# Batch 0 of a fused attention and gated-MLP kernel: split fp32r products in place of plain fp32 products

## The chip, the cores and the metric

The kernel runs on one core of one Trainium2 chip. The metric is the device time of one execution in microseconds (us), as the median of several runs of the same program.

## The reference

Eight batches; q, k and v are given per batch for 8 heads, 576 positions and 64 channels. Each batch goes through an attention that adds two parts, and the sum, with heads side by side as 512 channels, goes through a gated MLP with a residual:

```python
out_d = sm_attn(q_d, k_d, v_d)                    # q, k, v averaged over groups of 4 positions
mask = np.abs(pos[:, None] - pos[None, :]) < 4    # the local part: a band
...
x = repeat(out_d, 4) + softmax_band(q, k) @ v     # (8, 576, 512)
h = gelu_tanh(x @ w_in)                           # w_in: 512 x 1024
u, v = h[..., :512], h[..., 512:]
v_n = (v - mu) / np.sqrt(var + 1e-06) * g_ln
v_s = np.einsum('ts,bsd->btd', w_sg, v_n) + b_sg[None, :, None]
return x + (u * v_s) @ w_out                      # w_out: 512 x 512
```

The two large weights arrive as 64-bit floats and are turned into fp32 on the chip.

## The kernel before, in words

**Units of work.** The attention of a batch is done for four pairs of heads, so there are 32 pairs, numbered g = 4b + p. Pair g leaves its result in a tile of 128 channels by 576 positions, `x`, in the transposed form that the MLP needs; pair p of a batch is also slice k = p of the MLP's 512 input channels. The MLP of a batch has these products on TensorE: `v` (five blocks of positions, s = 0 to 4, the last of 64 positions; 512 columns), `u` (eight blocks of 288 columns), `s` (the product with w_sg) and `o` (the product with w_out).

**Split products.** A product of fp32 accuracy is made of fp32r matmuls: each operand is cut into a high part (a cast to fp32r) and a low part (the value minus its high part, again fp32r), and high by high, high by low and low by high are added in PSUM. For `x` this is `x_high` (task `xh`, ScalarE or VectorE), `x_low` (`xl`, VectorE or GpSimd, two SBUF inputs) and `x_last` (`xc`, which puts the low part of the last 64 positions behind the high part, so that the last block of `v` needs two matmuls per slice and not three). For a weight it is `high` (`wh`) and `low` (`wl`), behind the steps that make fp32 out of the 64-bit words: `scaled` and `units` (`wq`, `wu`, ScalarE), `shift` (`wb`, two VectorE operations) and `total` (`wt`, GpSimd).

**Batch 0.** Before the change, batch 0 has no `xh`, `xl` and `xc`. Its `v` and `u` take the plain fp32 `x` and the plain fp32 weights, as `total` leaves them (line 937 for `v`, line 1156 for `u`); such a matmul shows as two records in the trace. The weights are split all the same, but only batch 1 reads the parts. So that TensorE can begin before all four pairs of batch 0 are there, its `v` is cut into one task per slice: `vk`s`.`k for k = 0 to 2, and `v0.`s for k = 3. From batch 1 on, `v` runs on line 944 and `u` through `product` (line 1145).

**Order of the work.** A task list (name, engine, what it must follow, buffers) is written out by hand in Python, and a long string, `ORDER`, gives the order of all tasks; `/P`, `/V`, `/A` behind a name put it on GpSimd, VectorE or ScalarE in place of its usual engine. Each engine runs its tasks in that order and waits by semaphores. Other task names used below: `S`, `Y`, `YS` scores; `mx`, `my` row maxima; `ia`, `ib` scores minus their maximum; `ea`, `eb`, `ec` exponentials; `np`, `nq` the division by the row sums; `T`, `U`, `t` transposes; `D` the product with v; `qs`, `ks`, `vs` sums over four positions; `od`, `xa`, `xb` the sum of the two parts into `x`; `vg`, `vb`, `vp`, `vn`, `vh`, `vl` the GELU, the statistics, the root, the normalisation and the split of v. Where `vl` is done for all five blocks of batch 0, the first `s` product of batch 0 can start.

The program opens with 28 matmuls on zeros ahead of `S0` and has 20 more ahead of `S3`.

```python
if first:                                   # batch 0, in v_mm
    for k in ks:
        l = sb[k]["x"][:, s * P:min(S, (s + 1) * P)]
        nc.tensor.matmul(out=acc[0:LEFT] if last else acc, lhsT=l, rhs=unsplit(f"y{k}"), start=k == 0, stop=k == KT - 1)
    return
ops = []                                    # every other batch
for k in ks:
    xh, xl = sb[k]["xh"][:, ts], None if last else sb[k]["xl"][:, ts]
    ops += [(xh, 0, k), (xh, 1, k)] + ([] if last else [(xl, 0, k)])
```

Of the kernel before, what the change touches and what calls it, by code (L numbers as in the profile page):

```python
# [1540 lines left out]
```

## Time and profile before

| what | value |
|---|---|
| time, median of 3 runs | 547.8 us (546.92 to 550.19) |
| the profiled execution's own time | 548.28 us |
| its span, first to last instruction | 546.5 us |
| TensorE busy | 538.8 us (99% of the span) |
| VectorE busy | 461.3 us (84%) |
| ScalarE busy | 423.9 us (78%) |
| GpSimd busy | 346.0 us (63%) |

The busy times come from one profiled execution. TensorE's matmuls are pipelined and their ends are modelled, so its busy share says that it had work, not that it ran at its peak; where it says that TensorE is busy, the start of one matmul after another is the better measure. Shares over the whole span are averages over stages that have different limits.

### The profile page before, as it was taken

Reading aid. Unit: us, or ns where it says so; the run is one execution under the profiler, and the core shown is the slowest. Engines: PE = TensorE matmul, PEld = TensorE weight load, DVE = VectorE, ACT = ScalarE, POOL = GpSimd, SP = SyncE. Lnnn points to the kernel's source line nnn. Section 1 sums busy time; section 2 is a strip of 40 time slices with the busy share of each in tenths; the row PEclk is TensorE's granted clock in tenths of the full one; section 3 lists DMA queues with packets and bytes.
Section 4 is the critical chain, followed back from the end, with each engine's and each line's share of the span. In section 5 each row is a group of like instructions: output and inputs, shape, how many; then the busy total and the mean of one; then the engine's idle time right before and its main releaser. Section 6 shows DMA issues by size and latency. Waiting matters only on the chain.

```text
span 546.5 us, 17297 instructions
## 1 busy us (share of the span) xinstructions
PE 538.8 (99%) x6725; PEld 490.4 (90%) x6725; DVE 461.3 (84%) x994; ACT 423.9 (78%) x1447; POOL 346.0 (63%) x419
## 2 busy tenths in 40 slices
PE   9899999999999999999999999999999999999997
PEld 6746689899998999989998999989999899989997
DVE  5998999998889887897878888996998888975785
ACT  3999999798998987789797988797884987736320
POOL 6888878776796587576585654536545665544514
PEclk9999999999999999999999999999999999999999
DMA  8799466502443252303524242222435013200103
GB/s 308 209 313 321 163 185 199 172 23 58 137 124 90 88 189 76 111 24 110 168 79 148 63 147 97 68 80 81 150 110 183 3 57 131 75 1 1 67 0 109
DMA packets 31841, 64.47 MB, mean 118 GB/s; under 512 B 3728, under 2 KB 4752, under 8 KB 31760
## 3 DMA queue, kind: packets, MB, share of 16 engines
q1 hardware_dynamic: 31760, 63.38, 37.3%
q8 instruction: 53, 0.87, 0.7%
q14 instruction: 28, 0.23, 0.1%
HBM read 53.92 MB, written 9.44 MB: 116 GB/s over the span
## 4 chain that ended last, share of the span: by engine, by line
PE 90%; DMA 5%; ACT 2%; DVE 1%; SPq 1%; issue 0%; ACTq 0%
PE ps L1145 22%; PE ps L1099 17%; PE ps L944 16%; PE ps L1280 14%; PE ps L813 3%; PE ps L829 3%; PE ps L752 3%; PE ps L937 3%; PE ps L645 3%; PE ps L761 2%; PE ps L666 2%; DMA weight_y<-in_w_in_dram 2%; PE ps L1156 2%; DMA weight_z<-in_w_in_dram 1%; DMA R<-in_qT_dram 1%; SPq L240 1%
## 5 line engine op out<-in xcount | busy, mean ns | idle before, releaser
L1145 PE MATMUL ps<-X,weight_z 128*128 128x288 f32 x448 | 95.3, 298 | 0.3 <-issue 0.3
L705 ACT ACTIVATE X<-X,nb 128x64 f32<-128x64 f32 x280 | 93.6, 339 | 0.5
L944 PE MATMUL ps<-weight_y,X 128*128 128x512 f32 x280 | 85.0, 397 | 0.4 <-ACT R L963 0.4
L1145 PEld LDWEIGHTS ps<-X,weight_z 128*128 128x128 f32 x448 | 73.6, 188 | 0.7 <-issue 0.5
L1145 PE MATMUL ps<-R,weight_z 128*128 128x288 f32 x224 | 66.0, 295 | 0.0
L944 PEld LDWEIGHTS ps<-weight_y,X 128*128 128x128 f32 x280 | 51.1, 188 | 11.2 <-ACT R L963 0.7
L1099 PE MATMUL ps<-wsg_h,R 128*128 128x288 f32 x266 | 57.7, 299 | 0.0
L1287 DVE TENSOR_TENSOR R<-ps,R 128x288 f32<-128x288 f32 x98 | 42.0, 450 | 14.9 <-PE ps L1280 14.4
L705 ACT ACTIVATION_READ_ACCUMULATOR X<-X,nb 128x1 f32 x280 | 53.4, 191 | 0.0
L1280 PE MATMUL ps<-R,weight_r 128*128 128x288 f32 x336 | 49.6, 296 | 0.0
L248 ACT CAST R<-R 128x512 fp32r<-128x512 f32 (+2 forms) x68 | 42.5, 641 | 7.2 <-POOL R L1054 3.9
L1280 PEld LDWEIGHTS ps<-R,weight_r 128*128 128x128 f32 x336 | 46.2, 188 | 0.7
L944 PE MATMUL ps<-weight_y,R 128*128 128x512 f32 x112 | 44.1, 394 | 0.0
L1099 PEld LDWEIGHTS ps<-wsg_h,R 128*128 128x128 f32 x266 | 43.6, 188 | 0.3
L248 ACT COPY R<-ps 112x288 f32<-112x288 f32 (+4 forms) x93 | 32.2, 391 | 14.3 <-PE ps L944 5.5
L1145 PEld LDWEIGHTS ps<-R,weight_z 128*128 128x128 f32 x224 | 42.2, 188 | 0.0
L1263 POOL TENSOR_TENSOR R<-R,R 128x576 fp32r<-128x576 f32 x18 | 26.3, 1472 | 23.4 <-DVE R L248 13.5
L741 POOL TENSOR_TENSOR X<-X,rc 128x640 f32<-128x640 f32 x22 | 28.8, 1309 | 15.7 <-DVE rc L738 15.6
L1179 ACT ACTIVATE R<-ps 128x288 f32<-128x288 f32 x64 | 24.3, 411 | 18.3 <-PE ps L1145 16.7
L1280 PE MATMUL ps<-R,R 128*128 128x288 f32 x252 | 37.4, 297 | 0.0
L727 ACT ACTIVATE pd<-ps,nbd 128x144 f32<-128x144 f32 x96 | 35.4, 377 | 1.1 <-DVE nbd L696 0.5
L1280 PEld LDWEIGHTS ps<-R,R 128*128 128x128 f32 x252 | 34.8, 188 | 0.9
(223 smaller groups left out, 1643.7 us busy)
## 6 DMA issues: line engine op xcount, KB each, us to landing
R<-in_v_dram SPq DMA_DIRECT2D x60, 224.0 KB, 3.0
X<-in_vw_dram SPq DMA_DIRECT2D x32, 320.0 KB, 4.4
R<-in_qT_dram SPq DMA_DIRECT2D x32, 293.0 KB, 3.8
R<-in_kT_dram SPq DMA_DIRECT2D x32, 293.0 KB, 3.2
out_dram<-R SPq DMA_DIRECT2D x28, 288.0 KB, 3.0
R<-in_w_sgT_dram SPq DMA_DIRECT2D x10, 288.0 KB, 5.3
weight_y<-in_w_in_dram SPq DMA_DIRECT2D x4, 512.0 KB, 6.2
weight_z<-in_w_in_dram SPq DMA_DIRECT2D x4, 512.0 KB, 6.4
```

The lines of the kernel that those rows point to most:

```text
L248: (nc.scalar.copy if e == "A" else ENG[e].tensor_copy)(**kw)
L645: nc.tensor.matmul(out=sp[i][os, c * KB:(c + 1) * KB], lhsT=q[hs, t * QB:t * QB + KB], rhs=k[hs, t * QB:t * QB + KB], start=not early, sto ...
L705: nc.scalar.activation(out=st["ms"][:, t, :], in_=src, func=AF.Exp, bias=st["nb"][:, t:t + 1], scale=scale, accum_out=sums[par][:, t:t + 1])
L727: nc.scalar.activation(out=pd[:, n], in_=st["sdv"][n].rearrange("p (c k) -> p c k", c=3), func=AF.Exp, bias=st["nbd"][:, n:n + 1], scale=s ...
L741: ENG[e].tensor_tensor(out=st["ms"], in0=st["ms"], in1=bc_last(st["rc"][:, 0:NT], KB), op=ALU.mult)
L944: nc.tensor.matmul(out=acc, lhsT=r32(l), rhs=r32(weights[f"y{k}"][:, 0, w]), start=(i == 0 and ks[0] == 0), stop=(i == len(ops) - 1 and ks ...
L1099: nc.tensor.matmul(out=s_bank(j, c), lhsT=r32(l), rhs=r32(r), start=first_in and i == 0, stop=i == len(ops) - 1, skip_group_check=not firs ...
L1145: nc.tensor.matmul(out=acc[:, 0:HALF], lhsT=r32(l), rhs=r32(r), start=(first and n == 0), stop=(last and n == len(ops) - 1))
L1179: nc.scalar.activation(out=gate(i), in_=at["ps", "m", b, "u", i][:, 0:HALF], func=AF.Gelu_apprx_tanh)
L1263: ENG[e].tensor_tensor(out=r32(gl[m]), in0=us[raws[m]], in1=gh[m], op=ALU.subtract)
L1280: nc.tensor.matmul(out=bank(j, c), lhsT=r32(l), rhs=r32(r), start=first and i == 0, stop=i == len(ops) - 1, skip_group_check=not first)
L1287: nc.vector.tensor_tensor(out=x, in0=bank(j, c), in1=x, op=ALU.add)
```

## The change

Batch 0 is treated like the other batches. `unsplit` and the three branches for batch 0 (in `v_mm`, `v_act` and `u_mm`) go; the early return that kept `xh`, `xl` and `xc` from pairs 0 to 3 goes; `v` of batch 0 waits for `xl` and `wly`, its `u` for `xl` and `wlz`; the last block of its `v` gets the copy and the addition (`va`, `vj`) that the other batches have. `ORDER` is written anew, all 32 pairs and all batches of it. Fourteen tasks are new: `xh0` to `xh3`, `xl0` to `xl3`, `xc0` to `xc3`, `va0.4` and `vj0.4`; none goes.

```diff
@@ attention
         add(N("xb"), {"V": 0.38}, merge(1), [N("od"), N("xa")], gives=[("ps", "o", g, 1)])
-        if b == 0:
-            return
         add(N("xh"), {"A": 0.64, "V": 0.4}, x_high, [N("xa"), N("xb")], takes=[("X", "xh", g)])
@@ mlp
-        xn = [f"{'xb' if first else 'xl'}{b * NPAIR + p}" for p in range(NPAIR)]
+        xn = [f"xl{b * NPAIR + p}" for p in range(NPAIR)]
@@ v_mm
-                if first:
-                    for k in ks:
-                        l = sb[k]["x"][:, s * P:min(S, (s + 1) * P)]
-                        nc.tensor.matmul(out=acc[0:LEFT] if last else acc, lhsT=l, rhs=unsplit(f"y{k}"), start=k == 0, stop=k == KT - 1)
-                    return
@@ u_mm
-                if first:
-                    acc = buf("ps", "m", b, "u", i)[:, 0:HALF]
-                    for k in range(KT):
-                        l = block(unsplit(f"z{k // 2 * 2 + d}"))[:, k % 2, ds]
-                        nc.tensor.matmul(out=acc, lhsT=l, rhs=sb[k]["x"][:, cs], start=k == 0, stop=k == KT - 1)
-                    return
@@ the tasks of v and u
-            w = [f"{'wty' if first else 'wly'}{i}" for i in range(KT)] if b < 2 else []
+            w = [f"wly{i}" for i in range(KT)] if first else []
...
-            if last and not first:
+            if last:
                 add(N("va", s), {"A": 0.58, "V": 0.6}, v_act(s), [N("v", s)], takes=[("R", "v", b, s)])
...
-            w = [f"{'wt' if first else 'wl'}{j}" for j in z] if b < 2 else []
+            w = [f"wl{n}{j}" for n in "z" for j in range(KT) if j % 2 == i // 4] if first else []
@@ ORDER, its first line before and now
-lq0 qs0/P lk0 S0 mx0 ia0 ib0 ks0/P lk1 lq1 S1 mx1 ea0 Y0 lq2 qs1/P ks1/P Y1 my0 ia1 ib1 es0 wy0 wqy0 ny0 ec0 lk2 S2 lq3
+lq0 qs0 lk0 ks0 S0 wz3 wqz3/V wy0 lq1 Y0 wuz3 lk1 S1 wqy0 mx0 wbz3 wtz3 wy2 ia0 ib0 ea0 ks1/P whz3 qs1/P Y1 wby0 wuy0
```

**GpSimd, around the moment when slice 3 of batch 0 is there for its `v`.** In the rows before, line 429 is `total` of a weight (y and z are the two halves of w_in, the number is the slice), 436 is `low` of a weight, 741 and 749 are `np` and `nq`, 507 is the low part of w_sg:

```order
L429 TENSOR_TENSOR R33_815<-R33_815,weight_z0_701 128x512
L741 TENSOR_TENSOR X6_627<-X6_627,rc0_108 128x640
L749 TENSOR_TENSOR pd0_101<-pd0_101,rc0_108 128x9x48
L429 TENSOR_TENSOR R26_736<-R26_736,weight_y2_455 128x512
L429 TENSOR_TENSOR R32_809<-R32_809,weight_z3_721 128x512
L429 TENSOR_TENSOR R37_867<-R37_867,weight_y3_730 128x512
L741 TENSOR_TENSOR X9_838<-X9_838,rc1_109 128x640
L507 TENSOR_TENSOR wsg_l_80<-R35_849,wsg_h_79 128x576
L436 TENSOR_TENSOR weight_z0_910<-R33_815,weight_z0_910 128x2x256
L749 TENSOR_TENSOR pd1_102<-pd1_102,rc1_109 128x9x48
L429 TENSOR_TENSOR R13_1022<-R13_1022,weight_z1_870 128x512
L436 TENSOR_TENSOR weight_z3_986<-R32_809,weight_z3_986 128x2x256
```

In the rows now the same lines are 430 (`total`), 437 (`low`), 739 and 747 (`np`, `nq`), and 627 and 628 are `vs`, 846 is `xl` and 249 is `xc`; the second row of line 846 is `xl3`:

```order
L846 TENSOR_TENSOR R1_932<-R35_823,X8_826 128x576
L739 TENSOR_TENSOR X5_656<-X5_656,rc0_108 128x640
L437 TENSOR_TENSOR weight_y3_944<-R28_764,weight_y3_944 128x512
L747 TENSOR_TENSOR pd0_101<-pd0_101,rc0_108 128x9x48
L627 TENSOR_TENSOR pairs_1002<-R3_955 112x2x128
L628 TENSOR_TENSOR vd0_99<-pairs_1002 112x128
L627 TENSOR_TENSOR pairs_1005<-R2_956 112x2x128
L628 TENSOR_TENSOR vd0_99<-pairs_1005 112x128
L249 CAST X8_826<-R1_932 128x64
L437 TENSOR_TENSOR weight_z2_788<-R22_660,weight_z2_788 128x2x256
L846 TENSOR_TENSOR R13_1070<-R4_1051,X2_1054 128x576
```

Before, the `v` products of slice 3 needed from this queue only `total` of weight_y3, behind 27 other tasks of GpSimd; now they need `low` of weight_y3 and `xl3`, and `xl3` stands behind 34 tasks.

**TensorE, the same products.** R26, R37 are the plain weights of slices 2 and 3, R2 and R6 the plain `x` of pairs 2 and 3, ps0, ps4, ps5, ps6 the sums of four blocks of `v`; 752 and 761 are transposes. Before:

```order
L752 MATMUL ps1_970<-turn_l_72,X6_627 128x122
L761 MATMUL ps1_970<-turn_p_73,pd0_101 112x112 x3
L752 MATMUL ps2_975<-turn_l_72,X6_627 128x122 x4
L937 MATMUL ps5_761<-R26_736,R2_924 128x512
L937 MATMUL ps4_759<-R26_736,R2_924 128x512
L937 MATMUL ps4_759<-R37_867,R6_989 128x512
L937 MATMUL ps5_761<-R37_867,R6_989 128x512
L937 MATMUL ps0_857<-R26_736,R2_924 128x512
L937 MATMUL ps0_857<-R37_867,R6_989 128x512
L761 MATMUL ps2_1018<-turn_p_73,pd0_101 112x112 x2
L937 MATMUL ps6_917<-R26_736,R2_924 128x512
L937 MATMUL ps6_917<-R37_867,R6_989 128x512
```

Now X1 with R6 and X2 with R13 are the high and low parts of pairs 2 and 3, and a row with "x2" is the high part by both parts of the weight:

```order
L935 MATMUL ps6_882<-weight_y2_484,R6_1022 128x512
L935 MATMUL ps5_773<-weight_y2_484,X1_1020 128x512 x2
L935 MATMUL ps5_773<-weight_y2_484,R6_1022 128x512
L759 MATMUL ps4_1062<-turn_p_73,pd0_101 112x112 x2
L935 MATMUL ps3_1065<-weight_y0_317,X6_673 128x512 x2
L935 MATMUL ps3_1065<-weight_y0_317,R25_675 128x512
L935 MATMUL ps0_934<-weight_y3_944,X2_1054 128x512 x2
L935 MATMUL ps0_934<-weight_y3_944,R13_1070 128x512
L935 MATMUL ps6_882<-weight_y3_944,X2_1054 128x512 x2
L935 MATMUL ps6_882<-weight_y3_944,R13_1070 128x512
L935 MATMUL ps5_773<-weight_y3_944,X2_1054 128x512 x2
L935 MATMUL ps5_773<-weight_y3_944,R13_1070 128x512
```

A product that was one fp32 matmul became three fp32r matmuls (two in the last block of `v`), and slice 3 comes at the end of the `v` blocks that are open, behind `xl3`.

**VectorE, the end of batch 0's `v` path, just ahead of its first `s` product.** Before, the four whole `vl` stood on GpSimd, and only `vl0.4` (line 1034, 64 partitions) and one of the low parts of w_sg (507) stood here:

```order
L248 CAST X2_1412<-R11_1372 128x576
L507 TENSOR_TENSOR wsg_l_80<-R22_1179,wsg_h_79 128x576
L248 CAST weight_z1_1461<-R13_1022 128x2x256
L1034 TENSOR_TENSOR R25_1466<-R31_1196,R25_1466 64x512
L609 TENSOR_REDUCE kd1_98<-R4_1472 128x144
L653 TENSOR_TENSOR X8_1507<-ps3_1485,mask_sb_70 128x256
```

Now line 1022 is `vl`, line 249 a cast, and four `vl` of 128 partitions stand on VectorE within ten rows:

```order
L607 TENSOR_REDUCE kd0_97<-R8_1508 128x144
L249 CAST R14_1517<-R9_1086 128x512
L1022 TENSOR_TENSOR R12_1519<-R9_1086,R14_1517 128x512
L249 CAST R24_1523<-R5_1092 128x512
L249 CAST X7_1529<-R19_1200 128x576
L1022 TENSOR_TENSOR R7_1531<-R15_1102,R27_1365 128x512
L1002 TENSOR_SCALAR R23_1210<-R23_1210,mv1_111,rs1_114 64x512
L249 CAST R10_1586<-R37_1391 128x512
L1022 TENSOR_TENSOR R11_1588<-R5_1092,R24_1523 128x512
L1022 TENSOR_TENSOR R33_1592<-R37_1391,R10_1586 128x512
```

`vl0.0` to `vl0.3` moved from GpSimd to VectorE, and `vl0.4` the other way.

## Rows read from the trace of the kernel before

**Rows 1.** Windows: us, busy of PE, PEld, DVE, ACT, POOL, PEclk, DMA, GB/s

```profile
15.00:20.00 5.00, 3.69 (x79) 3.03 (x75) 4.89 (x16) 4.38 (x14) 3.97 (x4) 1.00 0.73 223
...
35.00:43.20 8.20, 7.93 (x135) 5.25 (x136) 7.01 (x17) 7.94 (x38) 8.12 (x9) 1.00 1.05 297
43.20:79.10 35.90, 35.80 (x446) 23.94 (x445) 32.70 (x74) 33.91 (x90) 29.25 (x32) 1.00 0.68 218
79.10:100.60 21.50, 21.50 (x362) 21.09 (x356) 19.28 (x44) 20.40 (x95) 19.96 (x18) 1.00 0.65 194
...
168.00:546.50 378.50, 375.12 (x4305) 354.42 (x4304) 311.85 (x656) 277.01 (x935) 209.99 (x260) 1.00 0.28 88
```

**Rows 2.** Chain that ended last, from 108.13 us to the end, by line

```profile
by line: PE ps L1145 23.4%; PE ps L1099 21.6%; PE ps L944 19.7%; PE ps L1280 18.0%; PE ps L813 2.9%; PE ps L752 2.9%; PE ps L829 2.8%; PE ps L645 2.8%; PE ps L666 2.5%; PE ps L761 2.5%; PE ps L350 0.1%; DVE R L1287 0.1%; issue 0.1%
```

**Rows 3.** Groups by line (busy, mean ns, idle before): fp32 products of batch 0

```profile
L937 PE MATMUL ps<-R,R 128*128 128x512 f32 (+1 forms) x40 | 19.6, 607 | 0.9 <-ACT R L248 0.5 <-DVE R L836 0.3
...
L1156 PE MATMUL ps<-R,R 128*128 128x288 f32 x64 | 16.4, 410 | 0.0
```

**Rows 4.** Chain in order of time: start, us, what; fp32 above, fp32r below

```profile
43.17 5.16 PE ps L937 x12
...
59.72 7.96 PE ps L1156 x32
...
131.69 6.35 PE ps L1145 x48
...
483.60 11.11 PE ps L944 x48
```

**Rows 5.** Timeline of POOL: start, us, line, operation, names

```profile
21.84 0.67 POOL L612 TENSOR_TENSOR half<-R 128x288 f32<-128x288 f32 x1
22.59 0.43 POOL L613 TENSOR_TENSOR kd<-half 128x144 f32<-128x144 f32 x1
22.97 1.26 POOL L741 TENSOR_TENSOR X<-X,rc 128x640 f32<-128x640 f32 x1
...
34.08 0.67 POOL L629 TENSOR_TENSOR pairs<-R 112x256 f32<-112x256 f32 x1
...
36.29 1.30 POOL L429 TENSOR_TENSOR R<-R,weight_z 128x512 int32<-128x512 int32 x1
37.54 1.26 POOL L741 TENSOR_TENSOR X<-X,rc 128x640 f32<-128x640 f32 x1
38.76 0.91 POOL L749 TENSOR_TENSOR pd<-pd,rc 128x432 f32<-128x432 f32 x1
...
78.66 1.87 POOL L848 TENSOR_TENSOR R<-R,X 128x576 fp32r<-128x576 f32 x1
80.49 1.29 POOL L436 TENSOR_TENSOR weight_z<-R,weight_z 128x512 fp32r<-128x512 f32 x1
```

**Rows 6.** Groups by line, POOL: x_low and x_last

```profile
L848 POOL TENSOR_TENSOR R<-R,X 128x576 fp32r<-128x576 f32 x17 | 25.1, 1478 | 6.8 <-ACT X L248 6.1 <-DVE R L1034 0.6
...
L248 POOL CAST X<-R 128x64 fp32r<-128x64 f32 x13 | 4.1, 325 | 2.6 <-DVE R L848 2.5
```

**Rows 7.** Timeline of DVE: first row maximum, first shift of a weight, vl0.4

```profile
8.32 0.89 DVE L675 TENSOR_REDUCE stats<-ps 128x4 f32<-128x256 f32 x2 [4.75 <-PE ps L645]
...
13.39 0.68 DVE L419 TENSOR_SCALAR ps<-weight_y 128x512 int32<-128x512 int32 x1
...
77.73 1.51 DVE L1034 TENSOR_TENSOR R<-R,R 64x512 fp32r<-64x512 f32 x1 [0.39 <-ACT R L248]
```

**Rows 8.** Groups by line, DVE: all v_low operations

```profile
L1034 DVE TENSOR_TENSOR R<-R,R 128x512 fp32r<-128x512 f32 (+1 forms) x23 | 17.4, 765 | 2.2 <-ACT R L248 1.2 <-PE ps L813 0.8
```

**Rows 9.** Groups by line, ACT, 0 to 125 us: x_high

```profile
L248 ACT CAST X<-R 128x576 fp32r<-128x576 f32 x4 | 2.7, 673 | 0.0
```

**Rows 10.** Timeline of PE: the 28 and the 20 matmuls on zeros

```profile
1.03 6.09 PE L1472 MATMUL ps<-zeros 128*128 128x256 bf16 x28 [1.03 <-DVE mask_sb L312]
...
11.86 2.36 PE L1472 MATMUL ps<-zeros 128*128 128x256 bf16 x20
```

More of the change, by code (lines that the diff above doesn't have):

```diff
@@ new lines @@
+vk1.1 wqr2 lw3 D3 vs4 wbz1 U4 vk4.0 xh2 xl2 pa4/V xc1 vk0.2 nx5 wuz1 vk2.2 eb5 vk1.2 ea5 oe3/V od3 pb4/V xa3 xb3 xh3
+wlz2 wq0 whq0/V lq6 t4 vk3.0 re5 xl3/P wbr2 v0.0 pc4 pe4/V qs6 lw4 rc5 vg0.0 wtz1 v0.2 vg0.2 nq5 xc2 np5 v0.1 lq7 vg0.1
+D4 lk6 ks6 YS6 xc3/A vk4.1 vb0.2 vb0.1/A qs7 whz1 oe4/V my6 vk4.2 ny6/V vp0.1 wq1 ma6 mb6 vk3.1 mx6 od4 xa4 xb4 lw5 v0.4
+ec6 va0.4 lv5 vs5 nx6 wlz1 vj0.4 U5 T5 pa5/V pb5 pc5/V ea6 vk3.2 v0.3 lk7 ks7 t5 pe5/V u0.2 eb6 D5 wlq0 YS7 vb0.0 vp0.0
+ua0.2 oe5 wq2 whq2/V re6/V wlq2/V vn0.1/A vp0.2 vg0.4 ma7 wq4 whq4 wq3 whq1/V vh0.1 wr3 wlq1/V u0.3 lq8 rc6 my7 ua0.3
@@ L955, in emit @@
                 vact[s] = [v]
-                if s == NS - 1 and first:
-                    total = dict(accum_out=sum5[s][0:LEFT]) if by_scalar(s) else {}
-                    nc.scalar.activation(out=v[0:LEFT], in_=acc[0:LEFT], func=AF.Gelu_apprx_tanh, **total)
-                elif s == NS - 1:
+                if s == NS - 1:
                     copy(e, out=v[0:LEFT], in_=acc[LEFT:P])
@@ L1358, in mlp @@
                     add(f"vk{s}.{k}", {"T": c / KT}, v_mm(s, range(k, k + 1)),
[L1359 to L1360 removed]
+                        xn[k:k + 1] + w[k:k + 1] + (xc[k:k + 1] if last else []) + ([f"vk{s}.{k - 1}"] if k else []),
+                        takes=[] if k else [("ps", "m", b, "v", s)])
                 add(N("v", s), {"T": c / KT}, v_mm(s, range(k + 1, KT)),
[L1362 removed]
+                    xn[-1:] + w[-1:] + (xc[-1:] if last else []) + [f"vk{s}.{k}"], gives=xs)
             else:
@@ L1382, in mlp @@
         for i in range(2 * KT):
-            z = [f"z{j}" for j in range(KT) if j % 2 == i // 4]
-            w = [f"{'wt' if first else 'wl'}{j}" for j in z] if b < 2 else []
-            add(N("u", i), {"T": 1.651}, u_mm(i), xn + w, takes=[("ps", "m", b, "u", i)],
-                gives=[("R", "w", j) for j in z] if first else xs)
+            w = [f"wl{n}{j}" for n in "z" for j in range(KT) if j % 2 == i // 4] if first else []
+            add(N("u", i), {"T": 1.651}, u_mm(i), xn + w, takes=[("ps", "m", b, "u", i)], gives=xs)
             add(N("ua", i), {"A": 0.38}, u_act(i), [N("u", i), None if opens(i) else N("ua", i - (2 if small_o else 1))],
```

233 lines of the change are left out of this document (112 added, 121 removed).

## The prediction

> **What bounds the kernel now.** I read the chain of waits first, then the busy times by stretch, then the timelines of the first 80 us. From 108 us on the chain is TensorE and nothing else: every line of it but two entries of 0.1% is a TensorE line [rows 2]. From 79.1 to 100.6 us TensorE is busy for 21.50 of 21.50 us too, and from 168 us to the end for 375.1 of 378.5, the drain at the end included [rows 1]. So from 79.1 us, when the first `s` product of batch 0 starts, the kernel runs at TensorE's pace for 546.5 - 79.1 = 467.4 us. Before that, more than one engine is full. From 43.2 to 79.1 us TensorE is busy for 35.8 of 35.9 us, ScalarE for 33.9, VectorE for 32.7; from 35.0 to 43.2 us GpSimd is busy for 8.12 of 8.20 us and ScalarE for 7.94 [rows 1]. A 99% share of TensorE says little there: its fp32 products may fill time that other engines need anyway.
>
> **What goes.** Batch 0 has 40 fp32 records in `v` and 64 in `u` [rows 3]; their mean durations are modelled, so I take start to start from the chain: 5.16 / 12 = 0.43 us for a record of `v`, 7.96 / 32 = 0.249 us for one of `u`; a fp32r matmul of 288 columns takes 6.35 / 48 = 0.132 us, one of 512 columns 11.11 / 48 = 0.231 us [rows 4]. `v` was 40 x 0.43 = 17.2 us and becomes 4 x 12 + 8 = 56 matmuls, 13.0 us; `u` was 64 x 0.249 = 15.9 us and becomes 96 matmuls, 12.7 us. TensorE has 7.4 us less to do, all of it ahead of the first `s`.
>
> What TensorE does behind the first `s` is the same set of tasks as before: the two orders have the same TensorE tasks ahead of it, only otherwise arranged. So the time after is the moment of the first `s`, plus 467.4 us, plus any gaps that the new order brings later. The whole question is when the first `s` starts.
>
> **What is added, on GpSimd.** Slice 3 of batch 0's `v` needs `xl3`, and `xl3` stands behind 34 tasks of GpSimd where the old product stood behind 27. That queue can't begin before VectorE has done the first row maximum and the shift of weight z3, which the new order puts in front of it: the row maximum starts at 8.32 us and takes 0.89, the shift is two operations of 0.68 [rows 7], so 8.32 + 0.89 + 1.36 = 10.6 us (before, GpSimd started its sums earlier; two of them now go to VectorE). The 34 tasks, by start to start times: 7 `total` of 37.54 - 36.29 = 1.25 (8.8 us), 8 sums of 22.97 - 21.84 = 1.13 (9.0), 5 `np` of 38.76 - 37.54 = 1.22 (6.1), 2 `vs` of 36.29 - 34.08 = 2.21 (4.4), 7 `low` of 1.29 (9.0), one `nq` of 0.91 [rows 5]; 2 `xl` of 1.48 (3.0) and 2 `xc` of 0.33 (0.7) [rows 6]. That is 41.9 us, and `xl3` itself 1.5: 10.6 + 41.9 + 1.5 = 54.0 us at the earliest. In the kernel before, that product starts at about 43.2 us [rows 4].
>
> Behind it TensorE has left, before the first `s`: 24 `v` matmuls (5.6 us), all of `u` (12.7 us), and the attention work of the stretch. The latter is what 35.9 us hold beside 24 fp32 records of `v` (10.3) and all of `u` (15.9), so 9.7 us. Together 28.0 us, and the first `s` starts at 54.0 + 28.0 = 82.0 us, 2.9 us later than before: the shorter products give back less than the later start takes.
>
> **What is added, on ScalarE.** It gets four `xh` of 0.67 us at most [rows 9], one `xc` and the copy of the last `v` block, which no row shows; the bounds for these two are nothing (if they fall in a wait) and 0.7 us each, the price of a cast of the same kind of tile [rows 9], and I take half. That is 2.7 + 0.7 = 3.4 us before the first `s`. The tasks that change engine there go both ways (18 come, 21 leave) and I set them at zero. ScalarE has 2.0 us free in the 35.9 us before the first `s` [rows 1], so this path asks for 1.4 to 3.4 us more. It points the same way by its own sum. If the cover (ScalarE's 2.0 us of idle time) is gone, the upper end holds.
>
> **What is added, on VectorE.** `xl2`, `vj0.4` and four `vl` against one; an operation of this kind is 0.77 us [rows 8]. VectorE has 3.2 us free in the stretch [rows 1], and two sums over q and k that moved to it fall in its wait of 4.75 us before 8.32 us [rows 7]. I cost this at nothing; without that cover it is up to 4 x 0.77 = 3.1 us, and it cannot be a gain, since no VectorE task goes away.
>
> **The sum.** GpSimd and TensorE ask for +2.9 us, ScalarE for +1.4 to +3.4, side by side, not one on top of the other. Three full queues that hand to one another do not hide each other's waits. GpSimd's own sum holds no wait at all; before, it stood still for 0.1 us in 8.2 us at its fullest and for 6.6 in 35.9 us after it [rows 1], so over its 43 us the bounds for waits are 0.4 and 8.0 us. I take 1.0, nearer the full stretch, since it is the same work on the same queue; the upper end alone would give 558.8 us and stays for the range. First `s` at 83.0 us, +3.9. Gaps behind it lie between nothing, as before [rows 2], and 2.2 us, VectorE's free time in the 21.5 us behind the first `s` [rows 1], if the new order uses it up and VectorE becomes late there; I take 0.1, near the row on the chain. So +4.0 us on the profiled execution's span of 546.5 us: 550.5. That execution took 548.28 us, 0.5 us above the median of 547.8, so the median to expect is 547.8 + 4.0 = 551.8 us.
>
> **Rivals.**
>
> *The saving comes through.* If `xl3` kept pace and ScalarE's load were hidden, the first `s` would start 7.4 us earlier and the median would be 540.4 us. For it: TensorE is full from 43.2 us on [rows 1]. Against it: GpSimd's 41.9 us behind 10.6 us cannot shrink by 7 us or more without another assignment, and ScalarE would need 6 us that it hasn't. Chance 0.07.
>
> *VectorE and GpSimd hold each other up.* `vl0.4` took 1.51 us while a GpSimd `low` and an `xl` ran [rows 5, 7], and its kind takes 0.77 us on the mean [rows 8]; that `xl` took 1.87 us, its kind 1.48 [rows 5, 6]. The new order puts four `vl` on VectorE close to the end of the path, and three `xl` on GpSimd on the way. If each pays that price, 4 x 0.74 + 3 x 0.39 = 4.1 us come on top: +8.1 us, 555.9 us, slower. It decides from about half of them on. For it: both engines are full just there. Against it: the mean says that most such operations do not pay. Chance 0.20. The Trainium skill, in its page GPSIMD Engine Reference, section 1. Specifications, says that GpSimd's SBUF interfaces are shared with VectorE, and that instructions of VectorE with two SBUF inputs contend for them; `vl` is such an instruction, and the 1.51 us agree. By that rule alone every one of the four would pay whenever GpSimd works, which is this rival; the mean says that it is not so each time.
>
> *TensorE loses its clock.* The 28 opening matmuls on zeros took 6.09 us, the 20 later ones, of the same shape, 2.36 [rows 10]: 0.218 against 0.118 us, half the speed at the start of the program. In every stretch of rows 1 the granted clock is 1.00, the higher level, 2.4 GHz. Now TensorE has some 7 us of products fewer and 11 us more of waiting before 54 us. If it comes out of those waits at the lower level (1.2 GHz) once, it loses what the opening lost, 6.09 - 28 x 0.118 = 2.8 us: +6.8 us, 554.6 us. Chance 0.06. The page TensorE: Matmul & The Clock Gate of the Trainium skill, section HAM oscillation, says that waits between short bursts send the clock back each time; before, from 15 to 20 us TensorE had 3.69 us of work in 5.00 and kept 1.00 [rows 1], so the trace does not bear that rule out for waits of that size.
>
> That the change does not do what it says is ruled out: the order rows show the split products.
>
> **How the numbers follow.** Forecast 551.8 us, chance 0.64, with a range of its own of 548.5 to 554.5: the lower end is ScalarE's 1.4 us less 0.7 for pure luck in the waits, the upper end the forecast with 2.7 us more of GpSimd's waits. The saving 0.07, contention 0.20, clock 0.06, the rest (0.03) longer gaps late in the run. A measurement of this kernel can tell about 1% from no change, 542.3 to 553.3 us. Slower by over 1%: nine tenths of contention, most of the clock's and the rest's, and a tenth of the forecast's chance, 0.18 + 0.05 + 0.03 + 0.07 = 0.33. Faster: 0.07. Within: 0.60. The range leaves out the saving and the far end of contention: 547.0 to 557.0 us.
>
> **What would show it.** Right: in the profile after, `xl3` ends near 55 us with GpSimd full ahead of it, the first `s` starts near 83 us, TensorE has gaps between 15 and 55 us, and the chain from the first `s` on is TensorE alone, 467 us long. The two fp32 lines are gone, and TensorE's busy time ahead of the first `s` falls. Wrong: the first `s` before 79 us, or TensorE gaps of more than 1 us in all behind 110 us, or `vl` rows of 1.5 us one after another, or a granted clock below 1.00.

## The result, and the profile after

The changed kernel takes 552.33 us (median of 6 runs, 552.01 to 553.72) against 547.61 us (546.92 to 550.19) of the kernel before on the same chip: a ratio of 1.0081, 95% interval 1.0061 to 1.0100. It is 0.8% slower; 551.8 us had been forecast. The profiled execution took 552.58 us, its span is 550.5 us.

Windows of the changed kernel, columns as in [rows 1]:

```profile
10.00:38.90 28.90, 21.64 (x495) 17.40 (x495) 27.42 (x63) 26.18 (x86) 27.99 (x32) 0.88 0.95 298
...
15.00:20.00 5.00, 5.00 (x74) 3.78 (x73) 4.63 (x12) 4.82 (x17) 4.77 (x7) 0.59 0.90 314
35.00:43.20 8.20, 6.47 (x104) 5.03 (x96) 7.93 (x20) 7.33 (x36) 7.96 (x12) 0.79 1.06 303
43.20:81.61 38.41, 37.40 (x627) 33.27 (x625) 35.70 (x78) 36.63 (x112) 30.64 (x39) 1.00 0.69 205
...
168.00:550.50 382.50, 378.47 (x4423) 357.19 (x4421) 312.46 (x659) 281.08 (x946) 225.46 (x269) 1.00 0.28 87
```

Before 39 us TensorE has waits of 7.3 us in 28.9, while GpSimd is busy for 28.0 of 28.9. The same stretch of the kernel before:

```profile
10.00:38.90 28.90, 26.30 (x583) 19.20 (x577) 28.25 (x67) 27.37 (x101) 24.12 (x31) 1.00 0.90 271
```

There TensorE was busy for 26.3 us and GpSimd for 24.1. So the work changed places: what left TensorE stands on GpSimd's queue, ahead of the products. From 43.2 us to the first `s` TensorE is all but full in both kernels (37.4 of 38.4 us now, and [rows 1]).

GpSimd's queue, from its first task to `xl3` (line 846), in the timeline:

```profile
10.05 1.30 POOL L430 TENSOR_TENSOR R<-R,weight_z 128x512 int32<-128x512 int32 x1 [7.67 <-DVE R L422]
...
50.52 0.24 POOL L249 CAST X<-R 128x64 fp32r<-128x64 f32 x1
50.71 1.29 POOL L437 TENSOR_TENSOR weight_z<-R,weight_z 128x512 fp32r<-128x512 f32 x1
52.28 1.44 POOL L846 TENSOR_TENSOR R<-R,X 128x576 fp32r<-128x576 f32 x1 [0.27 <-ACT X L249]
53.66 1.32 POOL L430 TENSOR_TENSOR R<-R,weight_z 128x512 int32<-128x512 int32 x1
```

A bracket gives the idle time ahead of a row and what ended it. Between 10.05 and 52.01 us there is none: the 34 tasks take 41.96 us. TensorE's rows where slice 3 begins, and at the first `s`:

```profile
53.77 0.51 PE L935 MATMUL ps<-weight_y,R 128*128 128x512 f32 x1 [0.22 <-POOL R L846]
...
81.61 0.54 PE L1133 MATMUL ps<-wsg_h,R 128*128 128x288 f32 x2
```

The first `s` starts at 81.6 us, 2.5 us later than before (79.1). From there to the end it takes 550.5 - 81.6 = 468.9 us, against 467.4. That is 1.5 us more, and the waits of TensorE from 104 us on, by line, are just these:

```profile
PE ps L1262 <- ACT R L951: 0.5, 1, 0.5
PE ps L1133 <- DVE X L651: 0.4, 1, 0.4
PE ps L1262 <- DVE R L1245: 0.4, 1, 0.4
PE ps L1133 <- DVE R L1204: 0.2, 1, 0.2
```

So the 4.0 us of the spans are 2.5 us ahead of the first `s` and 1.5 us behind it. Counted from the first `s`, TensorE waits for 1.8 us now (these four and 0.3 us ahead of 104 us) and waited for 0.7 us before, so waits are 1.1 of the 1.5 us.

### The profile page after: what moved, and what is told of

Same layout as the page of the kernel before. It is cut to its first block, busy times and chain, and to the rows that moved or that the text cites. A ratio compares the mean times of both kernels' runs of the same rounds, so it can differ in the third digit from the quotient of the medians.

```text
span 550.5 us, 17422 instructions
## 1 busy us (share of the span) xinstructions
PE 534.8 (97%) x6773; PEld 497.9 (90%) x6773; DVE 464.5 (84%) x1002; ACT 427.9 (78%) x1443; POOL 356.8 (65%) x430
## 4 chain that ended last, share of the span: by engine, by line
PE 85%; DVE 5%; ACT 4%; POOL 2%; issue 1%; POOLq 0%; DVEq 0%; ACTq 0%
PE ps L1133 23%; PE ps L1087 17%; PE ps L935 16%; PE ps L1262 14%; PE ps L750 3%; PE ps L643 3%; PE ps L664 3%; PE ps L811 3%; PE ps L827 2%; PE ps L759 2%; ACT X L703 1%; ACT pd L725 1%; DVE R L422 1%; POOL weight_y L437 0%; DVE ps L420 0%
## 5 line engine op out<-in xcount | busy, mean ns | idle before, releaser
L1133 PE MATMUL ps<-X,weight_z 128*128 128x288 f32 x512 | 108.6, 297 | 0.8 <-ACT R L1161 0.8
L935 PE MATMUL ps<-weight_y,X 128*128 128x512 f32 x320 | 97.6, 399 | 0.0
L1133 PEld LDWEIGHTS ps<-X,weight_z 128*128 128x128 f32 x512 | 84.0, 188 | 1.2 <-ACT R L1161 0.9
L1133 PE MATMUL ps<-R,weight_z 128*128 128x288 f32 x256 | 75.5, 295 | 0.0
L935 PEld LDWEIGHTS ps<-weight_y,X 128*128 128x128 f32 x320 | 58.5, 189 | 11.8
L249 ACT CAST R<-R 128x576 fp32r<-128x576 f32 (+1 forms) x71 | 44.5, 645 | 10.9 <-POOL R L1042 4.1
L935 PE MATMUL ps<-weight_y,R 128*128 128x512 f32 x128 | 50.8, 397 | 0.2 <-POOL R L846 0.2
L739 POOL TENSOR_TENSOR X<-X,rc 128x640 f32<-128x640 f32 x28 | 36.2, 1294 | 20.8 <-DVE rc L736 19.2
L1133 PEld LDWEIGHTS ps<-R,weight_z 128*128 128x128 f32 x256 | 48.2, 188 | 0.1
L846 POOL TENSOR_TENSOR R<-R,X 128x576 fp32r<-128x576 f32 x22 | 32.3, 1472 | 9.3 <-ACT X L249 3.5
L249 ACT COPY R<-ps 112x288 f32<-112x288 f32 (+4 forms) x75 | 26.8, 395 | 11.2 <-DVE R L249 3.6
```

The source lines that it names most:

```text
L249: (nc.scalar.copy if e == "A" else ENG[e].tensor_copy)(**kw)
L739: ENG[e].tensor_tensor(out=st["ms"], in0=st["ms"], in1=bc_last(st["rc"][:, 0:NT], KB), op=ALU.mult)
L846: ENG[e].tensor_tensor(out=r32(st["xl"]), in0=st["x"][:, 0:S], in1=st["xh"][:, 0:S], op=ALU.subtract)
L935: nc.tensor.matmul(out=acc, lhsT=r32(l), rhs=r32(weights[f"y{k}"][:, 0, w]), start=(i == 0 and ks[0] == 0), stop=(i == len(ops) - 1 and ks ...
L1133: nc.tensor.matmul(out=acc[:, 0:HALF], lhsT=r32(l), rhs=r32(r), start=(first and n == 0), stop=(last and n == len(ops) - 1))
```

## The experiments

Three sets: what the parts do by themselves (runs 1 to 3, 9, 11), which engine is late ahead of slice 3 (runs 4 to 8), and whether TensorE's work matters there at all (runs 10, 12). Names of theories go through all of them. "First s" is the start of the first `s` matmul, "rest" the span less that; both are of one profiled execution. That execution lies 2.5 us below the median in run 3, 1.9 us above it in run 11, and within 1.1 us of it in the others. Each ratio is against the kernel before on the same chip.

| run | median us | ratio to before, 95% | first s | rest |
|---|---|---|---|---|
| before | 547.6 | | 79.1 | 467.4 |
| changed | 552.3 | 1.0061 to 1.0100 | 81.6 | 468.9 |
| 1 new order, old products | 558.4 | 1.0179 to 1.0237 | 88.2 | 468.3 |
| 2 old order, new products | 569.4 | 1.0370 to 1.0429 | 101.3 | 466.8 |
| 3 only `u` split | 556.8 | 1.0138 to 1.0197 | 86.5 | 466.0 |
| 4 zeros keep the clock | 553.5 | 1.0086 to 1.0139 | 82.3 | 468.5 |
| 5 load on GpSimd | 556.7 | 1.0132 to 1.0182 | 84.6 | 469.4 |
| 6 load on ScalarE | 555.6 | 1.0128 to 1.0159 | 85.2 | 468.5 |
| 7 load on TensorE | 554.4 | 1.0098 to 1.0140 | 84.0 | 468.4 |
| 8 work moved behind | 555.3 | 1.0123 to 1.0153 | 84.9 | 468.2 |
| 9 old order behind first `s` | 551.9 | 1.0060 to 1.0100 | 83.0 | 466.0 |
| 10 high parts only | 554.3 | 1.0095 to 1.0150 | 84.5 | 468.6 |
| 11 three `u` split | 551.6 | 1.0057 to 1.0097 | 83.3 | 468.4 |
| 12 as 10, one cast moved | 551.6 | 1.0051 to 1.0090 | 80.0 | 468.9 |

The changed kernel and runs 4 and 9 differ little or nothing ahead of the first `s`, and it lies at 81.6, 82.3 and 83.0 us in them: less than some 1.4 us is not told apart by that column. A part of this can be seen in the traces. GpSimd's queue begins behind VectorE's first row maximum and the shift of z3, and that moment is not the same in each execution: 10.05 us in the changed kernel, and in runs 4 and 9

```profile
10.84 1.29 POOL L430 TENSOR_TENSOR R<-R,weight_z 128x512 int32<-128x512 int32 x1 [8.45 <-DVE R L422]
```

```profile
10.71 1.29 POOL L431 TENSOR_TENSOR R<-R,weight_z 128x512 int32<-128x512 int32 x1 [8.33 <-DVE R L423]
```

In all runs with this order it lies between 9.76 us (run 12) and 10.84. Counted from there the first `s` comes 71.6 us later in the changed kernel, 71.4 in run 4 and 72.3 in run 9.

**Run 1: the new order with the old products.** The kernel before, with the changed kernel's ORDER less the 14 tasks; the edit of that ORDER at one of them:

```diff
-np2 YS4 ma4 mb4 wbz2 nq2/A lv1 wlz0 xh0 xl0/P T2
+np2 YS4 ma4 mb4 wbz2 nq2/A lv1 wlz0 T2
...
```

> The kernel before, with the new ORDER in place of its own: the 14 new tasks are left out, the GELU of batch 0's last v block stands where the copy and the addition stood, batch 0's products are plain fp32 as before. In the changed kernel TensorE is full from 38.9 us to the first s at 81.7 us (1.0 us of waits). Theory A (waits for GpSimd, VectorE and ScalarE ahead of 39 us use up what the shorter products save, TensorE bounds the rest): the 47 v matmuls left at 38.9 us become 34 records, 14.6 for 10.9 us, u is 3.2 us longer, waits of 1.0 to 2.7 us go: first s at 84 to 88 us, time 555 to 558 us, slower than the changed kernel. Rival B (the split itself costs the time: its x_low and x_high tasks on full queues): first s at 79 us or earlier, time 548 us or less. Behind the first s, this order's own gaps stay in both: about 468.8 us from there to the end, against 467.4 in the kernel before.

Measured: 558.4 us, first `s` at 88.2 us, 468.3 us behind it: theory A, just past the end of its range. Rival B (the split itself is dear) falls: in the new order the longer plain products cost 88.2 - 81.6 = 6.6 us, most of the 7.3 us that they are longer from 38.9 us on. (The traces have 53 `v` matmuls of the changed kernel behind that moment and 38 records of run 1, not the 47 and 34 of the expectation: 16.3 us for 12.2, and 3.2 us for `u`.)

**Run 2: the old order with the split products.**

```diff
-wty3 xa3 wz2 vk0.2 why2 xb3 rc5 v0.0 why3
+wty3 xa3 wz2 why2 wly2 why3 wly3 vk0.2 vk3.2 xb3 xh3 xl3/P xc3/A rc5 v0.0
...
```

> The changed kernel's products with the old ORDER: the 14 tasks are put in right behind the pair or block they belong to, and the high and low parts of weights y2, y3, z1, z2 come forward behind their totals, as they must; two v tasks and one u task move behind them. Theory A: slice 3 waits on GpSimd for two low parts of weights (2.6 us), three x_low (4.3) and two x_last (0.5) more than before, so it starts near 43.2 + 7.4 = 50.6 us instead of 43.2, and the first s comes 28.0 us later, at 78.6 us plus up to 2 us of waits: 546.5 to 550 us. Rival C (the new arrangement of all the tasks is what costs, and the split would pay in the old one): first s at 75 us or earlier, time under 544 us. Rival B (the split itself is dear): over 552 us.

Measured: 569.4 us, 19 us above the end of theory A's range, and rival C falls with it. The two longest of TensorE's waits:

```profile
PE ps L936 <- POOL weight_y L438: 7.1, 2, 6.4
PE ps L751 <- POOL X L740: 5.5, 1, 5.5
```

A sum of durations on GpSimd's queue (7.4 us) was a poor forecast: a low part of a weight came with its chain of load, shift and cast in front, which stood late, and everything behind it in the queue waited too. This arrangement, put in by hand, says nothing against the split; that it loses almost five times as much as the changed kernel (22.5 us for 4.7, each against the kernel before on its chip) suggests what the new order was needed for.

**Run 3: only `u` split, in the old order.**

```diff
-xb3 rc5 v0.0
+xb3 xh1 xl1/P xh0 xl0/P rc5 v0.0 xh3 xl3/P xh2/V xl2
...
-wqz2 wtz1 vg0.2
+wqz2 wtz1 whz1/V wlz1 vg0.2
...
```

> The kernel before, with only batch 0's u as split products and its v plain fp32; x_high and x_low of pairs 0 to 3 stand between the v of slice 3 and the first u, two x_high on ScalarE and two on VectorE, x_low on GpSimd but one on VectorE; the parts of weights z1 and z2 come forward. Theory A: v keeps its early start, since it needs no part of GpSimd's queue that is new; u is 64 x 0.249 - 96 x 0.132 = 3.2 us shorter, and the 5 tasks more on GpSimd have 6.6 us of idle time in the 36 us ahead of the first s: first s at 76 to 78 us, time 544.5 to 547 us. Rival B (x_low and x_high cost what they take, 4 x 0.67 on ScalarE with 2.0 us free): no gain, 547 to 550 us.

Measured: 556.8 us, a miss for theory A and for rival B, whose range ended at 550. VectorE's timeline, a cast of weight z1 that was brought forward:

```profile
55.57 0.43 DVE L250 CAST weight_z<-R 128x512 fp32r<-128x512 f32 x1 [7.08 <-POOL R L431]
```

VectorE stood for 7.1 us at a cast that nobody needed yet, and TensorE 5.2 us for what was queued behind it. The run shows the price of an early wait in a queue, and tells nothing of the split `u` by itself.

**Run 4: zeros for the clock.**

```diff
-WARM = {"S0": 28, "S3": 20}
+WARM = {"S0": 28, "Y1": 20, "S3": 20, "U3": 4, "YS5": 8}
```

> The changed kernel with 32 more matmuls on zeros in TensorE's waits: 20 ahead of Y1 (wait of 2.81 us at 11 to 13.8 us), 4 ahead of U3 and 8 ahead of YS5 (waits of 0.65 and 1.08 us at 36.5 to 38.9 us). In the changed kernel the granted clock is 0.50 from 12.4 to 19.0 and from 39.6 to 43.0 us. Both theories expect 1.00 there, or a shorter drop. Theory A (GpSimd's queue, which is full from 10.05 us until x_low of pair 3 starts at 52.28): the wait of 0.27 us for x_high goes and no more, first s at 81.2 to 81.7 us, time 551.8 to 552.4 us. Rival D (the lower clock costs the time: TensorE works from 38.9 us on without a wait, 3.4 us of it at half speed, and the chain of waits goes through it): first s 1.7 to 2.5 us earlier, at 79.2 to 80.0 us, time 549.8 to 550.7 us.

Windows, the changed kernel first and run 4 below (the granted clock is the third figure from the right):

```profile
12.00:14.00 2.00, 0.21 (x4) 0.21 (x8) 2.00 (x6) 1.97 (x6) 1.79 (x4) 0.57 1.06 405
16.00:18.00 2.00, 2.00 (x57) 1.78 (x51) 1.97 (x5) 1.97 (x9) 1.84 (x4) 0.50 1.02 395
40.00:42.00 2.00, 2.00 (x35) 1.88 (x28) 1.83 (x6) 2.00 (x11) 1.92 (x4) 0.50 1.01 249
```

```profile
12.00:14.00 2.00, 1.76 (x17) 1.33 (x14) 1.97 (x5) 2.00 (x5) 1.84 (x4) 1.00 1.05 401
16.00:18.00 2.00, 1.60 (x55) 1.36 (x46) 1.97 (x4) 1.97 (x10) 1.76 (x4) 1.00 1.02 403
40.00:42.00 2.00, 2.00 (x57) 1.72 (x58) 1.97 (x6) 2.00 (x13) 2.00 (x3) 1.00 1.07 317
```

The clock stays at its higher level, 2.4 GHz, from 8 us to the first `s` of this execution, and nothing is won: 553.5 us, first `s` at 82.3. By itself the run does not separate the clock from the zeros: the last 8 of them held TensorE's scores back until 41.12 us, though VectorE's `od` was ready at 40.37. The executions of the changed kernel itself say more. Five had a mean granted clock of 0.991 and spans of 550.0 to 551.7 us; the sixth had 0.984, so more time at the lower level, and a span of 550.3. In run 9 three had 0.983 or 0.984 and spans of 548.8 to 550.0, three 0.991 to 0.994 and 550.2 to 551.9. The executions with more of the lower clock were not the longer ones. So rival D (the clock sets the time) falls; that at 1.2 GHz TensorE only filled time in which it would have waited is the likely reason, and not shown.

**Runs 5 to 7: 2.8 us more on one engine.**

```diff
@@ run 5, x_low
+            for _ in range(3 if g == 0 else 1):
@@ run 6, x_high
+            for _ in range(6 if g == 2 else 1):
@@ run 7
+WARM = {"S0": 28, "S3": 20, "vk0.0": 24}
```

> The changed kernel with x_low of pair 0 done three times over on GpSimd (it starts at 33.21 us; 2 x 1.38 us start to start = 2.8 us more ahead of x_low of pair 3). Theory A: GpSimd does not wait from 10.05 us until 52.0 us, and x_low of pair 3 waited 0.27 us for its x_high, so it starts about 2.5 us later, at 54.8 us; TensorE has 28.0 us behind it: first s at 83.9 to 84.5 us in place of 81.68, time 554.7 to 555.5 us by the changed kernel's 552.3. Rival E (one queue alone sets the first s, and it is not GpSimd's): first s at 82.0 us or earlier.

> The changed kernel with x_high of pair 2 done six times over on ScalarE (it starts at 46.95 us; 5 x 0.56 us = 2.8 us more, on the stretch where the chain of waits runs along ScalarE to x_high of pair 3). Theory A (ScalarE, GpSimd and TensorE are full side by side there, each one late by itself): x_high of pair 3 comes 2.8 us later, x_low 2.5 us later, first s at 83.9 to 84.5 us, time 554.7 to 555.5 us. Rival E (GpSimd's queue alone sets it): first s at 81.7 to 82.3 us, time within 0.6 us of the changed kernel's.

> The changed kernel with 24 matmuls on zeros ahead of vk0.0 (at 44.4 us; 24 x 0.118 = 2.8 us). Theory A: TensorE works without a wait from 38.9 us until slice 3 (0.22 us there), so its own queue is as late as the others and the whole load counts: first s at 84.0 to 84.5 us, time 554.8 to 555.5 us. Rival E (TensorE waits on GpSimd's or ScalarE's queue, so work put in ahead of slice 3 is hidden): first s at 81.7 to 82.3 us, time as the changed kernel's, 552.0 to 552.9 us.

Measured: first `s` +3.0, +3.5 and +2.4 us, and +2.8, +3.4 and +1.8 counted from the start of GpSimd's queue. GpSimd and ScalarE pass their load on whole, TensorE a good part of it, and rival E (one queue alone) falls. Two of the loads are not pure: in run 6 VectorE's `xl2` also waited 3.46 us behind the six casts, and in run 7 the granted clock stayed at 1.00 from 18 us on, which gives TensorE back up to 1.7 of the 2.8 us. In run 7 the load goes round: TensorE late, then VectorE and ScalarE late for pair 3, and GpSimd waits (its and ScalarE's timelines):

```profile
53.73 0.68 ACT L249 CAST X<-R 128x576 fp32r<-128x576 f32 x1 [2.73 <-DVE R L834]
...
54.49 1.43 POOL L846 TENSOR_TENSOR R<-R,X 128x576 fp32r<-128x576 f32 x1 [2.12 <-ACT X L249]
```

**Run 8: work moved behind slice 3.** Nothing is left out.

```diff
-xb3 xh3
-wlz2 wq0 whq0/V lq6 t4 vk3.0 re5 xl3/P wbr2
+xb3 wbz1 xh3 wq0 whq0/V lq6 t4 vk3.0 re5 xl3/P wuz1 wqr2 wur2 vs4 wlz2 wbr2
...
```

> The changed kernel relieved ahead of slice 3 on all engines at once: low part of z2 and the v sums of pair 4 (4.5 us of GpSimd) behind x_low of pair 3, three steps of weights z1 and r2 (1.7 us of ScalarE) and the shift of z1 (1.4 us of VectorE) behind pair 3 as well, and the 32 zeros of the fourth run that keep TensorE's clock. Nothing is taken away, it is only moved. Theory A: x_low of pair 3 starts at 50 to 51.3 us in place of 52.28, and the first s comes 0.5 to 2 us earlier if the stretch behind it (ScalarE busy for 26.0 of 27.0 us there) can take the moved work, at 79.7 to 81.2 us: 550.3 to 551.8 us. Rival F (what is moved comes back behind slice 3): x_low earlier but first s at 81.5 us or later, time 552 us or more.

Measured: 555.3 us and first `s` at 84.9, rival F's side, though `xl3` did not even come earlier. GpSimd's timeline:

```profile
53.08 1.44 POOL L847 TENSOR_TENSOR R<-R,X 128x576 fp32r<-128x576 f32 x1 [3.86 <-ACT X L250]
```

GpSimd stood free for 3.9 us and gained nothing: `xh3` came no earlier (52.33 us, 51.52 in the changed kernel), since the sums of pair 3 on VectorE, which it waits for, were late themselves, behind waits of 0.92 and 0.83 us for TensorE. The moved work had to be done in the full stretch behind: from the end of `xl3` to the first `s` it took 30.4 us, by 27.9 in the changed kernel.

**Run 9: the old order behind the first `s`.** A theory of its own, for the 1.5 us.

```diff
-YS8 vh0.4 my8 vl0.4/P s0.1 ma8 mb8 nx7 sa0.1 eb7 ea7 lv7 vs7 od6
...
+YS8 vh0.4 my8 vl0.4/P wqr1 wbr1 wur1 nx7/V xh5/V lv7 ma8 mb8 s0.0 s0.3
...
```

> The changed kernel up to its first s of batch 0, and from there on the tasks that are left in the old order. The new order takes 468.8 us from the first s to the end (468.2 to 469.4 in the runs with it), the old one 467.4 (466.0 and 466.8 in two others). Theory A (the gaps behind the first s belong to the new arrangement of the later tasks): first s unchanged at 81.5 to 82.0 us, 466.5 to 467.6 us behind it, time 550.3 to 551.5 us. Rival G (they come from what the change leaves undone at the first s): 468.5 us or more behind it, time 552 us or more.

Measured: 466.0 us behind the first `s`, and TensorE does not wait once from 84 us to the end. So the later gaps belong to the new arrangement of the later tasks; rival G falls. The first `s` came at 83.0 us, which theory A did not expect, and the median is no better (551.9). TensorE was at the lower clock for longer, in the changed kernel first and here:

```profile
32.00:44.00 12.00, 10.19 (x224) 8.52 (x227) 11.68 (x26) 10.88 (x47) 11.77 (x15) 0.86 1.05 295
```

```profile
32.00:44.00 12.00, 11.31 (x183) 10.11 (x184) 10.07 (x23) 11.01 (x45) 11.77 (x15) 0.57 1.06 322
```

The 1.4 us can be found in GpSimd's queue: it began 0.66 us later, and it waited for 0.27 us (a cast of weight y3 on ScalarE) and 0.83 us (`xh3`), where the changed kernel has one wait of 0.27. `xl3` starts at 53.68 us, 1.40 later. Whether the lower clock made ScalarE late there is open.

**Run 10: high by high only.** The two low products of batch 0's `v` and `u` are left out, so its output is not of fp32 accuracy.

```diff
-ops += [(xh, 0, k), (xh, 1, k)] + ([] if last else [(xl, 0, k)])
+ops += [(xh, 0, k)] if first else [(xh, 0, k), (xh, 1, k)] + ([] if last else [(xl, 0, k)])
...
```

> The changed kernel without the two low products of batch 0's v and u: high by high alone, 20 matmuls for 56 in v and 32 for 96 in u (8.3 + 8.4 us less TensorE); the low parts are still made and waited for. Theory A (ScalarE and GpSimd are as late as TensorE ahead of slice 3, and ScalarE is busy for 26.0 of 27.0 us behind it): x_low of pair 3 starts within 1 us of 52.28 us, and the first s comes no more than 4 us earlier, 77.7 to 81.7 us; time 548.5 to 552.5 us. Rival H (TensorE alone sets the pace from 38.9 us on): first s 12 to 15 us earlier, at 66 to 70 us, time 537 to 541 us.

Measured: TensorE has 16.8 us less to do, and the first `s` starts at 84.5 us, 2.9 us later than in the changed kernel; 554.3 us. `xl3` starts at 51.98 us as expected. Rival H (TensorE alone sets the pace) falls by some 15 us, and theory A's own range missed as well. The cause shows on VectorE. Its cast of the first part of w_sg, and GpSimd at the same time:

```profile
50.71 4.23 DVE L249 CAST wsg_h<-R 128x576 fp32r<-128x576 f32 x1
```

```profile
50.75 1.28 POOL L437 TENSOR_TENSOR weight_z<-R,weight_z 128x512 fp32r<-128x512 f32 x1
51.98 1.41 POOL L846 TENSOR_TENSOR R<-R,X 128x576 fp32r<-128x576 f32 x1
53.34 1.28 POOL L430 TENSOR_TENSOR R<-R,weight_z 128x512 int32<-128x512 int32 x1
```

The cast ends at 54.94 us, 0.32 us after the third of three GpSimd operations that ran back to back. In the changed kernel the same cast takes 1.57 us, from 50.75 to 52.32:

```profile
50.75 1.57 DVE L249 CAST wsg_h<-R 128x576 fp32r<-128x576 f32 x1
```

There it ends 0.32 us after GpSimd's low part of z2 (50.71 + 1.29), mostly in the 0.27 us for which GpSimd waits for `xh3`. The two other casts of w_sg on VectorE in that trace take 0.45 us each.

**Run 12: the same, with that cast on ScalarE.** It does run 10 over without the cast.

```diff
-whq0/V
+whq0/A
```

> The tenth run's kernel (batch 0's v and u high by high alone, 16.8 us less TensorE), with one cast of w_sg's first high part moved from VectorE to ScalarE. In the tenth run that cast took 4.23 us on VectorE, while three operations of GpSimd ran back to back until 0.32 us before its end; in the changed kernel 1.57 us, until 0.32 us after a GpSimd operation ended; elsewhere 0.45 us. Theory A with contention (the cast stood still for GpSimd, and VectorE's queue behind it set the first s): the first s comes 2.5 to 4 us earlier than the tenth run's 84.5, at 80.5 to 82 us, still within 1.5 us of the changed kernel's 81.7 though TensorE has 16.8 us less to do; time 550.5 to 552.5 us. Rival H (TensorE's products set the pace, and the cast alone hid that): first s at 76 us or earlier, time under 547 us. Rival I (the cast waited for its data, which ScalarE would wait for just as long): first s at 83.5 us or later.

Measured: first `s` at 80.0 us, 4.5 us earlier than in run 10 (a little more than expected; 0.45 of them from GpSimd's queue, which began earlier), 551.6 us, 2.8 below run 10's median; rivals H and I fall. With 16.8 us of matmuls less, the first `s` comes 1.6 us before the changed kernel's. The windows of 38.9 to 54.0 and 54.0 to 81.7 us, of the changed kernel and then of run 12:

```profile
38.90:54.00 15.10, 14.88 (x216) 11.99 (x217) 13.96 (x29) 13.86 (x57) 14.51 (x19) 0.89 1.03 315
54.00:81.70 27.70, 26.91 (x475) 24.96 (x474) 25.92 (x61) 26.28 (x74) 20.36 (x28) 1.00 0.56 157
```

```profile
38.90:54.00 15.10, 12.52 (x243) 9.87 (x244) 13.89 (x30) 14.41 (x57) 14.79 (x19) 0.84 1.02 316
54.00:81.70 27.70, 21.31 (x372) 17.97 (x365) 24.66 (x60) 26.78 (x78) 19.67 (x29) 0.84 0.56 166
```

TensorE now waits for 6.4 us in the second stretch, while ScalarE is busy for 26.8 of 27.7. One thing stands beside it: the granted clock was 0.50 three more times, for some 10 us between 52 and 77 us. As an estimate from the granted clock, 10 us at half speed cost up to 5 us of TensorE's work, so up to 5 of the 15 us that did not come through may have gone there; no run keeps the clock in this kernel. The waits of TensorE, 8.6 us from 38.9 us to the first `s` by 1.0 in the changed kernel, are read from the trace and stand without that estimate.

**Run 11: three blocks of `u` split, in the old order.** A try at a kernel faster than both.

```diff
-                if first:
+                if first and i not in (0, 1, 3):
                     acc = buf("ps", "m", b, "u", i)[:, 0:HALF]
...
```

> The kernel before, with three of the eight u blocks of batch 0 (0, 1 and 3, put last) as split products, all else plain fp32: 3 x (8 x 0.249 - 12 x 0.132) = 1.2 us less TensorE. Four x_high (two on ScalarE, two on VectorE) and four x_low (three on GpSimd, one on VectorE) come into the old order where these engines waited, and the low parts of weights y2 and y3, which only batch 1 reads, move behind the first s. Theory A (a shorter product pays where the low parts are ready before TensorE comes to it): first s at 77.9 to 78.5 us in place of 79.1, time 0.6 to 1.2 us below the kernel before. Rival B (each added operation on the full queues costs what it takes): first s at 79.5 us or later, no gain or a loss.

Measured: 551.6 us, first `s` at 83.3: rival B's side. TensorE waited 1.8 us for a ScalarE copy and 1.4 us for VectorE's sums of masked scores, ahead of the first `s`, where it had not waited before. The profiled execution (553.5 us) lies 1.9 us above the median, and its granted clock was 0.50 from about 82 to 85.5 us, so a typical first `s` of this run is likely earlier and its rest shorter. No version here beats the kernel before.

## Why the prediction was right, and where it was not

The time was right by 0.5 us, but in part by luck: two terms of the sum missed in opposite directions by the same 1.4 us, the first `s` (+2.5 us for +3.9) and the gaps behind it (+1.5 for +0.1).

**GpSimd's queue: right.** The step put the 34 tasks at 41.9 us from 10.6 us on, and the end of `xl3` at 54.0. They took 41.96 us from 10.05 us on (a start that differs by about 1 us from run to run), and `xl3` ended at 53.72. The price of the waits in that queue was mis-sized: +1.0 us was taken, 0.27 came. That and the earlier start make the first `s` +2.5 us, not +3.9.

**"TensorE has left 28.0 us" behind slice 3: the number right, its meaning not.** From 53.77 to 81.61 us it is 27.8 us. But the step took this for TensorE's time. Runs 10 and 12 took 16.8 us of TensorE's work away and won 1.6 us at best (up to 5 us more may have gone to the lower clock), while run 1 put 7.3 us on and lost 6.6: at such a balance more counts nearly in full and less counts for little. ScalarE (26.3 of 27.7 us busy there in the changed kernel) needs the stretch as well, and products that end sooner only wait. The saving of 7.4 us was gone before that: by 38.9 us TensorE had used it up, in more waits (7.3 us from 10 us on, 2.6 before) and at the lower clock (12.4 to 19.0 us), and had as much to do until the first `s` as before (before 79.1 - 38.9 = 40.2 us; now 42.7 less 1.0 of waits and some 1.7 at half the clock).

**ScalarE, side by side with GpSimd and not on top: right.** Runs 5, 6 and 7 moved the first `s` by 3.0, 3.5 and 2.4 us for 2.8 us on each engine, and run 8 gained nothing from relieving several at once. VectorE was not loaded by itself, so its cost "at nothing" is not tested; in run 8 its sums of pair 3 were the last to come, but behind waits for TensorE. What sets the moment of the first `s` is thus no single queue, and no arrangement that gives it back was found.

**Gaps behind the first `s`: wrong in size.** 0.1 us was taken, "near the row on the chain" of the kernel before, with 2.2 as the upper bound. It was 1.5, of which 1.1 are waits; run 9 shows that the new arrangement of the later tasks makes them. The four waits behind 104 us, 1.5 us in all, are also more than the 1 us that had been named as a sign of being wrong. A chain of waits without gaps says that the old order had hardly any, nothing of a new one.

**The clock: the sign of a wrong prediction appeared, and cost nothing that can be measured.** The granted clock was 0.50, the lower level of 1.2 GHz, from about 12.4 to 19.0 us and from 39.6 to 43.0 us. The first fall came in the midst of a wait of 2.81 us, when TensorE had been busy for 1.22 of the 4.00 us before; ahead of the second it had been busy for 2.27 of 4.00. The step had argued from 3.69 us of work in 5.00 [rows 1], with shorter waits. The Trainium skill's rule in TensorE: Matmul & The Clock Gate, section HAM oscillation, that waits between bursts send the clock back, agrees with this trace. The 2.8 us that the rival put on it did not come: run 4 kept the clock and won nothing, and executions with more of the lower clock were no longer.

**Contention: there, but not where it was put.** The four `vl` on VectorE took 0.67 us (one 0.77), not 1.5, and `xl` on GpSimd 1.42 to 1.44. But the rival was hardly put to the test there: GpSimd stood still from 77.2 to 80.8 us, while the last three of the four ran (77.44 to 80.11), and nothing in the prediction had counted on that. GpSimd's next task behind them:

```profile
80.78 1.27 POOL L1022 TENSOR_TENSOR R<-R,R 64x512 fp32r<-64x512 f32 x1 [3.58 <-ACT R L249]
```

In the kernel before, `vl0.4` (77.73 to 79.24 us) had met a `low` of GpSimd, not the one of [rows 5] at 80.49 but this:

```profile
77.42 1.28 POOL L436 TENSOR_TENSOR weight_z<-R,weight_z 128x512 fp32r<-128x512 f32 x1 [1.71 <-DVE weight_z L248]
```

It ended at 78.70, and `vl0.4` 0.54 us later. In the changed kernel the rival's mechanism struck a cast instead: 1.57 us for 0.45, and 4.23 in run 10. The Trainium skill, page SBUF — State Buffer, section Who interferes with whom, says that a VectorE operation in one of its two-port modes and a GpSimd operation shut each other out for the whole instruction and do not share. The 1.57 us agree (in which mode the cast ran, no run here shows); the 4.23 us, through three operations, are more than the one instruction that it speaks of.

## What to carry to other kernels

Where several engines are full side by side and hand to one another, shortening the work of the one that shows 99% can buy next to nothing, as here; add a few microseconds to each in turn, and take some away, before moving work between them. What leaves TensorE as shorter products comes back as casts and subtractions on queues that are read in order, and counts there from the first task that has to be early. A new order of the whole program is a change of its own: look at what it does far behind the place that it was written for.
